# Softmax-free attention denominators: from two TensorE products with a head mask to 32x32 block transposes on VectorE

## The chip, the core and the metric

The kernel runs on one core of one Trainium2 chip. The metric is the time of one execution in microseconds (us), as the device reports it. The core has a matrix engine (TensorE, PE in the profile), VectorE (DVE), ScalarE (ACT), GpSimd (POOL) and SyncE (SP, which here only issues transfers). Each runs its own instructions in order, and they wait for each other through semaphores. PE reads SBUF and writes PSUM; the other compute engines work on tiles of 128 partitions by some number of columns.

## The reference, cut to what matters

x is 2048 tokens by 448 features. Two branches are computed from it and mixed by a gate per token.

```python
g = sigmoid((x * gate_w).sum(-1, keepdims=True))
# linear attention, 16 heads of 28
phi = lambda t: where(t > 0, t + 1, exp(t)) + 1e-6
pq, pk = phi(q), phi(k)                       # q, k, v from x @ wqkv
kv  = einsum("bhsd,bhse->bhde", pk, v)
z   = einsum("bhsd->bhd", pk)
num = einsum("bhqd,bhde->bhqe", pq, kv)
den = einsum("bhqd,bhd->bhq", pq, z)[..., None] + 1e-6
a   = (num / den) @ wo
# dense block, 1792 hidden
r = relu(x @ w1 + b1); b = (r * r) @ w2 + b2
out = g * a + (1 - g) * b
```

The change is about `den`: for each token and head, the sum over the 28 features of the head of pq times z, plus 1e-6, inverted, and then multiplied onto pq.

## The kernel before, in words

**Number format.** Every matrix product is made of two or three float32r products: each operand is split into a rounded high part and the rest (`split_hi` on line 63, mostly on ACT; `split_lo` on line 71, mostly on DVE), and high by high, high by low and low by high are accumulated in one PSUM bank. So each tensor that PE reads has passed an ACT copy and a DVE subtraction.

**Order.** PE, ACT and DVE run exactly in the order in which the program is written (line 170); a small list `todo` (`run_todo`, line 530) holds steps that are written one stage later than the products they follow. Tokens go in four blocks of 512 (TB); the hidden features in 14 chunks of 128, seven (NH) in a first half and seven in a second. The first half of the program runs blocks 0 to 3 over hidden chunks 0 to 6 together with the keys. The second half (line 684 on) runs blocks in the order 3, 0, 1, 2, which the loop calls n = 0 to 3, over hidden chunks 7 to 13, which it counts as fl = 0 to 6. In each stage (n, fl) PE does `up` (line 241: 11 products into `h_ps`), then `down` of the chunk before (line 260: 12 products into the four `o_ps` accumulators; `leave` holds back the last one or two of them until the next `down`), and then queries or attention. `hidden` (line 231) stands behind each `up`: ACT Relu and Square (`hr`), DVE cast (`hh`) and DVE subtraction (`hl`); `down` of that chunk one stage later needs `hh` and `hl`.

**Queries and denominators.** `queries(b, c)` (line 449) makes 128 rows of q per chunk c for 512 tokens: rows are features, columns tokens. Chunks 0 to 2 hold 24 features per head, chunk 3 the other four. A head has eight of the 128 rows in each chunk. Chunk 3 holds two partial sums per feature on separate partitions, which are swapped between partitions by eight small DMAs (`swap`, line 470, four issued on SP and four on POOL) and added (`join`, line 478). After phi (`qe`), the step `after` multiplies each row by its z (`zc`) and sums the four chunks into `ds`, 128x512: eight partial sums per head, one on each of the head's rows. From there:

- `split_den` (line 483): ACT rounds `ds` to `dh`, DVE subtracts to `dl`.
- `denominators` (line 489): PE multiplies the constant 128x128 mask `hm` (1 where two rows belong to one head) by `dh` and by `dl`, which leaves the head's sum on each of its eight rows (`d_ps`); ACT adds 1e-6 and copies to `rec`; DVE inverts `rec` by four reciprocals of 128 columns (line 498) in the stage after.
- `scaled(b, c)` (line 501): DVE multiplies `qe` by `rec` (line 506), ACT rounds to `qh`, DVE subtracts to `ql`. Chunk 3 goes through `split_last` (line 76).
- `attention` (line 513): 11 products per tile of 128 tokens, of `qh`, `ql` and `m_s` (kv times wo), into `a_ps`; ACT applies the gate (`u`), DVE adds to `part`.

For n = 0 `split_den` stands in stage 4 ahead of `up`, the mask products at the end of stage 4, the reciprocals at the head of stage 5, and `scaled` in stages 5 (chunk 0) and 6 (chunks 1 to 3). For n = 1 to 3 `split_den` and the mask products stand in stage 0, the reciprocals at the head of stage 1 ahead of `hidden`, and `scaled` in stages 2 and 3, two chunks each, one chunk after the other. Attention of block n = 0 comes in stage 0 of n = 1; that of the others in stages 4 to 6.

**Buffers.** `slot` (line 54) gives one of 15 SBUF buffers of 512 columns, `bank` (line 48) one of two PSUM banks in turn, for `k_ps`, `g_ps`, `q_ps`, `d_ps` and `a_ps` alike. `hm` comes from a mask that is loaded in the first half (lines 663 to 665).

Of the kernel before, what the change touches and what calls it, by code (L numbers as in the profile page):

```python
# [7 lines left out]
F = mybir.dt.float32  # L8
R = mybir.dt.float32r
AF = mybir.ActivationFunctionType  # L10
# [4 lines left out]
DH = D // H  # L15
# [13 lines left out]

@with_exitstack  # L30
def gated_mix_kernel(ctx: ExitStack, tc: tile.TileContext, xw, xt, xn, wk, wq, wv, wo, w1a, w1b, w2, b1, b2, gw,
                     hmask, kvmask, halves, out):
    nc = tc.nc
    act, dve, pool, pe, sp = nc.scalar, nc.vector, nc.gpsimd, nc.tensor, nc.sync

# [12 lines left out]
    def bank(name):  # L48
        turn[0] ^= 1
        return ms_p.tile([P, 512], F, name=name, tag=f"ms{turn[0]}")  # L50
# [3 lines left out]
    def slot(shape, dt, name):  # L54
        return work.tile(shape, dt, name=name, tag="s", bufs=NSLOT)

    def load(dst, src):
        sp.dma_start(out=dst, in_=src)
# [4 lines left out]
    def split_hi(eng, hi, src):  # L63
        if eng is act:
            act.activation(hi, src, AF.Copy)  # L65
        elif eng is pool:
            pool.tensor_scalar(hi, src, 1.0, 0.0, op0=ALU.mult, op1=ALU.add)
        else:
            eng.tensor_copy(hi, src)  # L69

    def split_lo(eng, lo, src, hi):
        eng.tensor_tensor(lo, src, f32(hi), op=ALU.subtract)  # L72
# [8 lines left out]
    def products(out_ps, terms):  # L81
        n = len(terms)
        for i, (a, b) in enumerate(terms):
            pe.matmul(out_ps, a, b, start=(i == 0), stop=(i == n - 1))  # L84
# [119 lines left out]

    b2_s = keep.tile([P, D], F, name="b2_s")
    gw_s = keep.tile([P, D], F, name="gw_s")
    hm = keep.tile([P, 8 + P], R, name="hm")[:, 8:]
    dve.memset(ones, 1.0)
    ksum = keep.tile([P, D], F, name="ksum")

# [146 lines left out]
    def split_wq(c):  # L357
        raw = wq_raw.pop(c)
        split_hi(act, wq_s[:, c], raw)
        if c < 3:  # L360
            split_lo(dve, wq_s[:, 4 + c, :384], raw[:, :384], wq_s[:, c, :384])
        else:
            split_lo(dve, wq_s[64:, 3, :384], raw[64:, :384], wq_s[64:, 3, :384])
        second = [t[:, 384:].rearrange("p (j r) -> p j r", j=NJ)[:, :, 16:] for t in (wq_s[:, c], raw)]
        split_lo(dve, second[0], second[1], second[0])


# [4 lines left out]
    def key_sums():  # L372
        zk = slot([P, 4, NJ, 32], F, "zk")
        ks = ksum.rearrange("p (j k) -> p j k", j=NJ)
        pool.memset(zk[:, 3], 0.0)
        pool.tensor_copy(zk[:, :3], ks[:, :, :96].rearrange("p j (c r) -> p c j r", c=3))
        pool.tensor_copy(zk[:, 3, :, :16], ks[:, :, 96:])
        zks.append(zk)
        act.activation(gate[:, 0], logit, AF.Exp, scale=-1.0)
        dve.tensor_scalar_add(gate[:, 0], gate[:, 0], 1.0)  # L380
        dve.reciprocal(gate[:, 0], gate[:, 0])
        dve.tensor_scalar(gate[:, 1], gate[:, 0], -1.0, 1.0, op0=ALU.mult, op1=ALU.add)
# [49 lines left out]
    def m_product(j):  # L432
        wh, wl = wo_s.pop(j)
        ps = mm_p.tile([P, 512], F, name=f"m_ps{j}", tag="mm")
        products(ps[:, :D], [(kv[0][:, j], wh), (kv[0][:, j], wl), (kv[1][:, j], wh)])
        m = late.tile([P, 2, D], R, name=f"m{j}", tag="m", bufs=1)
        split_hi(act, m[:, 0], ps[:, :D])
        split_lo(dve, m[:, 1], ps[:, :D], m[:, 0])

        p = j * 32  # L440
        for c in range(3):
            pool.dma_start(out=m_s[p:p + 32, c::4][:, :2], in_=m[c * 32:c * 32 + 32])
        pool.dma_start(out=m_s[p:p + 16, 3], in_=m[96:112, 0])
        pool.dma_start(out=m_s[p + 16:p + 32, 3], in_=m[112:, 1])


    pq, qs, den = {}, {}, {}
# [1 line left out]
    def queries(b, c):  # L449
        ps = bank(f"q_ps{b}_{c}")  # L450
        xh, xl = xs[b]
        cols = slice(c * P, (c + 1) * P)
        if c < 3:
            products(ps, terms_w(xh, xl, wq_s, cols))
        else:
            products(ps, [(wq_s[:, i, cols], x[:, i]) for i in range(4) for x in ((xh, xl) if i < 3 else (xh,))])
        e = slot([P, TB], F, f"qe{b}_{c}")
        r = slot([P, TB], F, f"qr{b}_{c}")
        v = slot([P, TB], F, f"qv{b}") if c == 3 else None
        pq[b, c] = e  # L460

        def after():
            phi(ps if c < 3 else v, e, r, e)
            if (b, "s") not in den:
                den[b, "s"] = slot([P, TB], F, f"ds{b}")
                dve.tensor_scalar(den[b, "s"], e, zc[:, c:c + 1], None, op0=ALU.mult)
            else:
                dve.scalar_tensor_tensor(den[b, "s"], e, zc[:, c:c + 1], den[b, "s"], op0=ALU.mult, op1=ALU.add)

        def swap():  # L470

            act.copy(v, ps)  # L472
            for p in range(0, P, 32):
                load(r[p:p + 16], v[p + 16:p + 32])
                pool.dma_start(out=r[p + 16:p + 32], in_=v[p:p + 16])  # L475
            return [join]

        def join():
            dve.tensor_tensor(v, v, r, op=ALU.add)
            after()  # L480
        return [swap if c == 3 else after]

    def split_den(b):
        den[b, "h"], den[b, "l"] = slot([P, TB], R, f"dh{b}"), slot([P, TB], R, f"dl{b}")
        total = den.pop((b, "s"))
        split_hi(act, den[b, "h"], total)
        split_lo(dve, den[b, "l"], total, den[b, "h"])

    def denominators(b):
        ps = bank(f"d_ps{b}")  # L490
        products(ps, [(hm, den.pop((b, "h"))), (hm, den.pop((b, "l")))])
        den[b, "r"] = rec = slot([P, TB], F, f"rec{b}")

        act.activation(rec, ps, AF.Copy, bias=1e-6)

        def part_(i):
            for j in range(2 * i, 2 * i + 2):
                dve.reciprocal(rec[:, j * P:(j + 1) * P], rec[:, j * P:(j + 1) * P])
        return [lambda: part_(0), lambda: part_(1)]

    def scaled(b, c):
        p = pq.pop((b, c))
        h = late.tile([P, TB], R, name=f"qh{b}_{c}", tag="q", bufs=NLATE)
        lo = late.tile([P, TB], R, name=f"ql{b}_{c}", tag="q", bufs=NLATE)
        qs[c] = (h, lo)
        dve.tensor_tensor(p, den[b, "r"], p, op=ALU.mult)
        if c < 3:
            split_hi(act, h, p)
            split_lo(dve, lo, p, h)
        else:  # L510
            split_last(h, lo, p, half)

    def attention(b, i):
        t = 4 * b + i
# [104 lines left out]
    for b in range(1, NB):  # L619
        for f in range(NH):  # L620
# [36 lines left out]
            if b == 2:  # L657
                if f < 4:
                    load_wq(f)
                if 1 <= f < 5:  # L660
                    split_wq(f - 1)
                if f == 5:
                    raw = slot([P, P], F, "hmr")
                    pool.dma_start(out=raw, in_=hmask)
                    split_hi(act, hm, raw)
                    load(half, halves)
            if b == 3:
                if f < 4:
# [18 lines left out]
    for n, b in enumerate(order):  # L687
        then = order[n + 1] if n + 1 < NB else None
        for f in range(NF - NH, NF):
            fl = f - NH  # L690
            run_todo()
            if fl == (0 if n else 4) and n != 1:
                split_den(b)
            up(b, f)
            if then is not None and n and fl < 2:
                load_x(then, 2 * fl)
                load_x(then, 2 * fl + 1)
# [21 lines left out]
            if fl:  # L719
                if n + 1 < NB or f + 2 < NF:  # L720
                    down(b, f - 1, leave=leaves[n][fl])
                elif f + 1 < NF:
                    down(b, f - 1, range(3))
                    down(b, f - 1, [3], leave=leaves[n][fl], end=NH - 3)
            elif n == 0:
                down(b, NH - 1)
                half_done(b)
            else:
                down(order[n - 1], NF - 1)
                for i in range(4):  # L730
                    if n == 1:
                        attention(order[0], i)
                        if i == 1:
                            split_den(b)
                    finish(order[n - 1], i)
            if n == 0:
                if fl in (2, 3):
# [14 lines left out]
                    m_product(2)  # L752
                if fl == 5:
                    m_product(3)
                for c in ((0,), (1, 2, 3))[fl - 5] if fl >= 5 else ():
                    scaled(b, c)
                if fl >= 4:
                    for c in ((3,), (0,), (1, 2))[fl - 4]:
                        todo += queries(then, c)
                if fl == 4:  # L760
                    todo += denominators(b)
            else:
                if fl == 0:
                    todo += denominators(b)
                if 2 <= fl < 4:
                    scaled(b, 2 * fl - 4)
                    scaled(b, 2 * fl - 3)
                for i in (((0,), (1,), (2, 3)) if then is not None else ((0, 1), (2,), (3,)))[fl - 4] if fl >= 4 else ():
                    attention(b, i)
                if then is not None and 3 <= fl:  # L770
# [71 lines left out]
```

## Time and profile before

| what | value |
|---|---|
| time, median of 3 runs | 435.01 us |
| lowest and highest of them | 434.67 and 435.04 us |
| profiled execution, first to last instruction (its span) | 432.7 us |
| median less that span: start and end of the program | 2.3 us |
| granted TensorE clock in the profile | 1.000 |
| ACT busy, share of the span | 174.8 us, 40% |
| POOL busy, share of the span | 72.0 us, 17% |

The profile records the span of one execution and no time of its own around it; the 2.3 us are the difference to the median. "L254" is line 254 of the kernel; a line can be that of a helper, so tiles tell more than lines. Busy times of PE overlap, because a product is counted until its modelled end while the next is already running; the distance from start to start of two products is what one costs.

### The profile page before, as it was taken

What the parts mean: (1) busy time and instruction counts of PE and PEld (TensorE: products, weight loads), DVE (VectorE), ACT (ScalarE), POOL (GpSimd) and SP (SyncE); (2) the same over time, 40 slices, a digit from 0 to 9 for tenths busy, and PEclk for the clock granted to TensorE, in tenths of its full rate; (3) what the DMA queues carried; (4) which work ended last, traced back from release to release, by engine and by line L of the source; (5) the groups of instructions that cost most, each with busy time, mean ns of one, the idle gap of its engine ahead of it and who ended that gap; (6) DMA issues with size and microseconds to landing.
All of it is one profiled execution on the core that took longest, in us unless ns stands there. A gap on an engine that the chain in (4) does not pass through costs nothing.

```text
span 432.7 us, 5576 instructions
## 1 busy us (share of the span) xinstructions
PE 428.9 (99%) x2058; PEld 380.6 (88%) x2058; DVE 284.7 (66%) x464; ACT 174.8 (40%) x304; POOL 72.0 (17%) x93
## 2 busy tenths in 40 slices
PE   9999999999999999999999999999999999999997
PEld 6889999898989899898898888988888888888986
DVE  5999518843499337884459777887653966457624
ACT  6855324521346133453145543444433534233421
POOL 0055006500065002540010441000100001000000
PEclk9999999999999999999999999999999999999999
DMA  8842302120232211223245321130101401002002
GB/s 284 240 134 63 96 0 71 24 68 5 65 89 63 68 45 48 66 59 110 65 117 144 72 63 38 63 120 0 26 0 46 139 0 27 0 0 86 0 2 85
DMA packets 18411, 29.11 MB, mean 67 GB/s; under 512 B 2896, under 2 KB 12736, under 8 KB 18384
## 3 DMA queue, kind: packets, MB, share of 16 engines
q1 hardware_dynamic: 16480, 26.46, 20.1%
q0 software_dynamic: 1760, 2.20, 2.3%
q8 instruction: 16, 0.26, 0.3%
q14 instruction: 11, 0.09, 0.1%
q10 hardware_dynamic: 144, 0.10, 0.1%
HBM read 22.43 MB, written 3.67 MB: 60 GB/s over the span
## 4 chain that ended last, share of the span: by engine, by line
PE 99%; DVE 0%; issue 0%
PE h_ps L229 32%; PE o_ps L254 31%; PE q_ps L84 8%; PE a_ps L84 8%; PE g_ps L84 8%; PE k_ps L254 8%; PE kv_ps L404 1%; PE warm_ps L177 1%; PE m_ps L84 1%; PE d_ps L84 0%; PE last L84 0%; PE h_ps L549 0%; PE z_ps L398 0%; DVE last L786 0%
## 5 line engine op out<-in xcount | busy, mean ns | idle before, releaser
L254 PE MATMUL o_ps<-w,hh 128*128 128x448 f32 x444 | 127.9, 362 | 0.0
L229 PE MATMUL h_ps<-xh,w 128*128 128x512 f32 x390 | 124.7, 390 | 0.0
L254 PEld LDWEIGHTS o_ps<-w,hh 128*128 128x128 f32 x444 | 83.2, 187 | 7.6
L229 PE MATMUL h_ps<-xl,w 128*128 128x512 f32 x224 | 86.7, 389 | 0.0
L229 PEld LDWEIGHTS h_ps<-xh,w 128*128 128x128 f32 x390 | 73.1, 188 | 14.7 <-DVE w L72 0.4
L254 PE MATMUL o_ps<-w,hl 128*128 128x448 f32 x222 | 80.4, 362 | 0.0
L233 ACT ACTIVATE hr<-h_ps,b_s 128x512 f32<-128x512 f32 x56 | 38.1, 680 | 85.8 <-PE h_ps L229 80.3
L69 DVE CAST hh<-hr 128x512 fp32r<-128x512 f32 x56 | 23.5, 420 | 61.3 <-ACT hr L234 61.1
L229 PEld LDWEIGHTS h_ps<-xl,w 128*128 128x128 f32 x224 | 42.0, 188 | 7.9
L254 PEld LDWEIGHTS o_ps<-w,hl 128*128 128x128 f32 x222 | 41.6, 188 | 3.7
L72 DVE TENSOR_TENSOR hl<-hr,hh 128x512 fp32r<-128x512 f32 x56 | 39.6, 707 | 3.4
L72 POOL TENSOR_TENSOR nl<-xnr,nh 128x384 fp32r<-128x384 f32 x16 | 17.2, 1075 | 119.0 <-ACT nh L65 118.9
L234 ACT ACTIVATE hr<-hr 128x512 f32<-128x512 f32 x56 | 35.4, 632 | 1.8
L84 PE MATMUL q_ps<-xh,wq_s 128*128 128x512 f32 x100 | 33.0, 389 | 0.0
L84 PE MATMUL a_ps<-m_s,qh 128*128 128x448 f32 x112 | 32.7, 362 | 0.0
L254 PE MATMUL k_ps<-wk_s,xh 128*128 128x448 f32 x112 | 32.7, 361 | 0.0
L475 POOL DMA_DIRECT2D qr<-qv x16 | 7.9, 503 | 124.3 <-ACT qv L472 94.5
L72 DVE TENSOR_TENSOR pl<-r,ph 128x448 fp32r<-128x448 f32 x16 | 23.7, 1479 | 0.0
L326 POOL TENSOR_TENSOR ksum<-ksum,r 128x448 f32<-128x448 f32 x15 | 23.3, 1554 | 1.1 <-DVE r L288 1.1
L84 PE MATMUL q_ps<-xl,wq_s 128*128 128x512 f32 x60 | 23.3, 389 | 0.0
L254 PE MATMUL k_ps<-wk_s,xl 128*128 128x448 f32 x64 | 23.2, 363 | 0.0
L84 PE MATMUL a_ps<-m_s,ql 128*128 128x448 f32 x64 | 23.2, 362 | 0.0
(118 smaller groups left out, 571.0 us busy)
## 6 DMA issues: line engine op xcount, KB each, us to landing
xr<-in_xt SPq DMA_DIRECT2D x27, 256.0 KB, 2.7
xnr<-in_xn SPq DMA_DIRECT2D x16, 224.0 KB, 2.6
out<-out SPq DMA_DIRECT2D x15, 224.0 KB, 2.0
w2r<-in_w SPq DMA_DIRECT2D x14, 224.0 KB, 2.7
w1r<-in_w1a SPq DMA_DIRECT2D x7, 256.0 KB, 2.8
w1r<-in_w1b SPq DMA_DIRECT2D x8, 192.0 KB, 3.3
m_s<-m POOLq DMA_DIRECT2D x12, 112.0 KB, 2.5
wqr<-in_wq SPq DMA_DIRECT2D x4, 256.0 KB, 2.7
```

The costliest lines, as they stand in the source:

```text
L69: eng.tensor_copy(hi, src)
L72: eng.tensor_tensor(lo, src, f32(hi), op=ALU.subtract)
L84: pe.matmul(out_ps, a, b, start=(i == 0), stop=(i == n - 1))
L177: pe.matmul(warm_ps[:, :256], warm[:, :P], warm, start=True, stop=True)
L229: pe.matmul(ps, a, m, start=(c == 0 and n == 0), stop=(c == 3 and n == 1))
L233: act.activation(r, ps, AF.Relu, bias=b1_s[:, f:f + 1])
L234: act.activation(r, r, AF.Square)
L254: pe.matmul(ps, a, m, start=start, stop=stop)
L326: pool.tensor_tensor(ksum, ksum, p, op=ALU.add)
L404: pe.matmul(kv_ps[:JE, js], wv_s[c][:, js], gsum[c][:, js], start=(c == 0), stop=(c == 3))
L475: pool.dma_start(out=r[p + 16:p + 32], in_=v[p:p + 16])
```

## The change

The 128x512 sums `ds` are no longer sent through PE. One step, `denominators`, does all: DVE transposes `ds` in 32x32 blocks (tokens now lie on partitions, the 32 rows of a block in columns), adds up groups of eight neighbouring columns (512 columns to 64: 16 blocks by four heads), adds 1e-6 and inverts on those 64 columns; ACT copies each of them eight times; DVE transposes back into the buffer of `ds`, which `scaled` then reads as the inverse. For this the eight rows of a head must be neighbours, so the host lays out the columns of the weights in another order, and the pairs of chunk 3 lie on even and odd partitions: the swap DMAs, the last two copies of `m_product`, one copy of `key_sums` and a subtraction in `split_wq` go in steps of two instead of runs of 16. The mask, its load and its rounding go.

`split_den` goes. `denominators` stands at the end of stage 4 for n = 0, and in stage 1 behind `up` (and so behind `hidden`) for n = 1 to 3. `scaled` now takes a pair of chunks: the product of the second chunk is written ahead of the subtraction of the first. For n = 0 the pairs stand in stages 5 and 6.

```diff
-    def split_den(b):
-        den[b, "h"], den[b, "l"] = slot([P, TB], R, f"dh{b}"), slot([P, TB], R, f"dl{b}")
-        total = den.pop((b, "s"))
-        split_hi(act, den[b, "h"], total)
-        split_lo(dve, den[b, "l"], total, den[b, "h"])
-
     def denominators(b):
-        ps = bank(f"d_ps{b}")
-        products(ps, [(hm, den.pop((b, "h"))), (hm, den.pop((b, "l")))])
-        den[b, "r"] = rec = slot([P, TB], F, f"rec{b}")
-
-        act.activation(rec, ps, AF.Copy, bias=1e-6)
-
-        def part_(i):
-            for j in range(2 * i, 2 * i + 2):
-                dve.reciprocal(rec[:, j * P:(j + 1) * P], rec[:, j * P:(j + 1) * P])
-        return [lambda: part_(0), lambda: part_(1)]
-
-    def scaled(b, c):
-        p = pq.pop((b, c))
...
+        total, turned = den.pop((b, "s")), slot([P, TB], F, f"dt{b}")
+        dve.transpose(turned, total)
+        heads = total[:, :TB // 8]
+        dve.tensor_reduce(heads, turned.rearrange("p (h k) -> p h k", k=8), axis=mybir.AxisListType.X, op=ALU.add)
+        dve.tensor_scalar_add(heads, heads, 1e-6)
+        dve.reciprocal(heads, heads)
+        act.activation(turned.rearrange("p (h k) -> p h k", k=8), heads.unsqueeze(2).to_broadcast([P, TB // 8, 8]),
+                       AF.Copy)
+        den[b, "r"] = total
+        dve.transpose(total, turned)
+
+    def scaled(b, chunks):
+        owing = None
+        for c in chunks:
+            p = pq.pop((b, c))
...
+            dve.tensor_tensor(p, den[b, "r"], p, op=ALU.mult)
+            if owing:
+                split_lo(dve, *owing)
+            owing = None
+            if c < 3:
+                split_hi(act, h, p)
+                owing = lo, p, h
+            else:
+                split_last(h, lo, p, half)
+        if owing:
+            split_lo(dve, *owing)
...
             for p in range(0, P, 32):
-                load(r[p:p + 16], v[p + 16:p + 32])
-                pool.dma_start(out=r[p + 16:p + 32], in_=v[p:p + 16])
+                load(r[p:p + 32:2], v[p + 1:p + 32:2])
+                pool.dma_start(out=r[p + 1:p + 32:2], in_=v[p:p + 32:2])
...
-            if fl == (0 if n else 4) and n != 1:
-                split_den(b)
             up(b, f)
+            if n and fl == 1:
+                denominators(b)
...
-                for c in ((0,), (1, 2, 3))[fl - 5] if fl >= 5 else ():
-                    scaled(b, c)
+                if fl >= 5:
+                    scaled(b, ((0, 1), (2, 3))[fl - 5])
...
                 if fl == 4:
-                    todo += denominators(b)
+                    denominators(b)
             else:
-                if fl == 0:
-                    todo += denominators(b)
                 if 2 <= fl < 4:
-                    scaled(b, 2 * fl - 4)
-                    scaled(b, 2 * fl - 3)
+                    scaled(b, ((0, 1), (2, 3))[fl - 2])
...
-    head = 4 * (p // 32) + p % 16 // 4
+    head = p // 8
```

More of the change, by code (lines that the diff above doesn't have):

```diff
@@ L31, in gated_mix_kernel @@
 def gated_mix_kernel(ctx: ExitStack, tc: tile.TileContext, xw, xt, xn, wk, wq, wv, wo, w1a, w1b, w2, b1, b2, gw,
-                     hmask, kvmask, halves, out):
+                     kvmask, halves, out):
     nc = tc.nc
@@ L206, in gated_mix_kernel @@
     gw_s = keep.tile([P, D], F, name="gw_s")
-    hm = keep.tile([P, 8 + P], R, name="hm")[:, 8:]
+    keep.tile([P, 8 + P], R, name="off")
     dve.memset(ones, 1.0)
@@ L363, in split_wq @@
             split_lo(dve, wq_s[64:, 3, :384], raw[64:, :384], wq_s[64:, 3, :384])
-        second = [t[:, 384:].rearrange("p (j r) -> p j r", j=NJ)[:, :, 16:] for t in (wq_s[:, c], raw)]
+        second = [t[:, 385::2] for t in (wq_s[:, c], raw)]
         split_lo(dve, second[0], second[1], second[0])
@@ L376, in key_sums @@
         pool.tensor_copy(zk[:, :3], ks[:, :, :96].rearrange("p j (c r) -> p c j r", c=3))
-        pool.tensor_copy(zk[:, 3, :, :16], ks[:, :, 96:])
+        pool.tensor_copy(zk[:, 3, :, ::2], ks[:, :, 96:])
         zks.append(zk)
@@ L442, in m_product @@
             pool.dma_start(out=m_s[p:p + 32, c::4][:, :2], in_=m[c * 32:c * 32 + 32])
-        pool.dma_start(out=m_s[p:p + 16, 3], in_=m[96:112, 0])
-        pool.dma_start(out=m_s[p + 16:p + 32, 3], in_=m[112:, 1])
+        pool.dma_start(out=m_s[p:p + 32:2, 3], in_=m[96:112, 0])
+        pool.dma_start(out=m_s[p + 1:p + 32:2, 3], in_=m[112:, 1])
     pq, qs, den = {}, {}, {}
@@ L501, in scaled @@
-    def scaled(b, c):
-        p = pq.pop((b, c))
[L503 to L511, printed above, removed]
+    def denominators(b):
+        total, turned = den.pop((b, "s")), slot([P, TB], F, f"dt{b}")
[8 more added lines that the diff above has]
+        dve.transpose(total, turned)
@@ new lines, in scaled @@
+    def scaled(b, chunks):
+        owing = None
+        for c in chunks:
+            p = pq.pop((b, c))
+            h = late.tile([P, TB], R, name=f"qh{b}_{c}", tag="q", bufs=NLATE)
+            lo = late.tile([P, TB], R, name=f"ql{b}_{c}", tag="q", bufs=NLATE)
+            qs[c] = (h, lo)
+            dve.tensor_tensor(p, den[b, "r"], p, op=ALU.mult)
[9 more added lines that the diff above has]
+            split_lo(dve, *owing)
@@ L662, in gated_mix_kernel @@
                 if f == 5:
-                    raw = slot([P, P], F, "hmr")
-                    pool.dma_start(out=raw, in_=hmask)
-                    split_hi(act, hm, raw)
                     load(half, halves)
@@ L732, in gated_mix_kernel @@
                         attention(order[0], i)
-                        if i == 1:
-                            split_den(b)
                     finish(order[n - 1], i)
@@ L802 @@
     p = np.arange(P)
-    head = 4 * (p // 32) + p % 16 // 4
-    q_of = np.stack([head * DH + c * 8 + p % 32 // 16 * 4 + p % 4 for c in range(3)] + [head * DH + 24 + p % 4])
-    k_of = np.concatenate([np.r_[q_of[:3, 32 * j:32 * j + 32].reshape(-1), q_of[3, 32 * j:32 * j + 16]]
+    head = p // 8
+    q_of = np.stack([head * DH + c * 8 + p % 8 for c in range(3)] + [head * DH + 24 + p % 8 // 2])
+    k_of = np.concatenate([np.r_[q_of[:3, 32 * j:32 * j + 32].reshape(-1), q_of[3, 32 * j:32 * j + 32:2]]
                            for j in range(NJ)])
-    hmask = (head[:, None] == head[None, :]).astype(np.float32)
     kvmask = (np.arange(JE)[:, None] // DH == k_of[None, :] // DH % 4).astype(np.float32)
-    halves = np.where(p[:, None] % 32 < 16, [[-1.0, 0.0]], [[1.0, 1.0]]).astype(np.float32)
+    halves = np.where(p[:, None] % 2 == 0, [[-1.0, 0.0]], [[1.0, 1.0]]).astype(np.float32)
     w1 = inputs["B_w1"][twice].reshape(4, P, 2, NH * P).transpose(2, 0, 1, 3)
@@ L828 @@
         "gw": inputs["gate_w"],
-        "hmask": hmask,
         "kvmask": kvmask,
```

## The prediction

> **What bounds the kernel now.** I read the busy shares first, then the chain of work that ended last, on the page.
>
> ```profile
> span 432.7 us, 5576 instructions
> PE 428.9 (99%) x2058; PEld 380.6 (88%) x2058; DVE 284.7 (66%) x464; ACT 174.8 (40%) x304; POOL 72.0 (17%) x93
> ...
> PE 99%; DVE 0%; issue 0%
> ```
>
> The chain is PE from end to end: TensorE runs product behind product, and no step of the chain is a wait for another engine. DVE is busy for two thirds of the span and idle for one. So a product taken from PE's list is worth what it occupies there, as long as no other engine becomes late; what DVE or ACT gain or lose is worth nothing by itself. Next, the same chain in order of time, for the block n = 2, and the operations of the removed tile.
>
> ```profile
> 335.85 0.45 PE d_ps L84 x2
> ...
> 338.80 2.21 PE o_ps L254 x11
> 341.00 2.49 PE h_ps L229 x11
> 343.50 2.21 PE o_ps L254 x11
> 345.70 2.49 PE h_ps L229 x11
> 348.19 2.81 PE o_ps L254 x14
> ...
> 357.49 2.20 PE a_ps L84 x11
> ```
>
> ```profile
> L84 PE MATMUL d_ps<-dh,hm x4: 388/388/389, 250.8 to 388.3; 128*128 128x512 f32 x4
> ...
> L84 PE MATMUL d_ps<-dl,hm x4: 389/389/389, 251.1 to 388.5; 128*128 128x512 f32 x4
> ```
>
> The reader is to see that one mask product lasts 0.39 us, but a pair takes only 0.45 us of the chain, since products overlap; and that the pieces join without a gap (343.50 + 2.21 = 345.71, the next starts at 345.70).
>
> **What PE gives back.** There are four pairs, one per block: 4 x 0.45 = 1.8 us. All four stand between other products in PE's list, none at an end. The span of the profiled execution becomes 432.7 - 1.8 = 430.9 us. The median of the runs is 2.3 us above that span (435.0 - 432.7), which I leave as it is: 433.2 us. This is the whole gain; the rest of this part asks whether it is lost again.
>
> **What DVE and ACT lose and gain in a block.** The rows of the operations concerned, grouped by line with shapes apart (count, then busy us and mean ns):
>
> ```profile
> L72 DVE TENSOR_TENSOR dl<-ds,dh 128x512 fp32r<-128x512 f32 x4 | 2.8, 691 | 2.1 <-ACT dh L65 2.1
> L498 DVE RECIPROCAL rec<-rec 128x128 f32<-128x128 f32 x16 | 13.5, 908 | 0.9 <-ACT rec L494 0.9
> L381 DVE RECIPROCAL gate<-gate 128x16 f32<-128x16 f32 x1 | 0.3, 252 | 0.0
> L380 DVE TENSOR_SCALAR gate<-gate 128x16 f32<-128x16 f32 x1 | 0.2, 168 | 0.0
> L72 DVE TENSOR_TENSOR pl<-r,ph 128x448 fp32r<-128x448 f32 x16 | 23.7, 1479 | 0.0
> L65 ACT ACTIVATE dh<-ds 128x512 fp32r<-128x512 f32 x4 | 2.5, 630 | 6.9 <-DVE ds L468 6.9
> L494 ACT ACTIVATE rec<-d_ps 128x512 f32<-128x512 f32 x4 | 2.4, 597 | 3.5 <-PE d_ps L84 3.5
> L468 DVE SCALAR_TENSOR_TENSOR ds<-qe,zc,ds 128x512 f32<-128x512 f32 x12 | 9.0, 752 | 0.4
> ```
>
> ```profile
> 338.80 3.38 DVE L498 RECIPROCAL rec<-rec 128x128 f32<-128x128 f32 x4
> 342.09 0.36 DVE L69 CAST hh<-hr 128x512 fp32r<-128x512 f32 x1
> 342.49 0.69 DVE L72 TENSOR_TENSOR hl<-hr,hh 128x512 fp32r<-128x512 f32 x1
> 343.10 1.28 DVE L72 TENSOR_TENSOR xl<-xr,xh 128x512 fp32r<-128x512 f32 x2
> ```
>
> Removed per block: the subtraction `dl` (0.69 us) and four reciprocals (3.38 us) on DVE, the rounding `dh` (0.63 us) and the copy `rec` (0.60 us) on ACT. Added, none of it in this trace but the kinds of the two small ones:
>
> - Two transposes and one reduction, each passing 512 columns. The nearest rows with 512 columns at both ends are the cast (0.36 us) and the subtraction (0.69 us); the slowest DVE pace of the trace is the reciprocal's, (908 - 252) / 112 = 5.9 ns a column, or about 3.2 us for 512. I take 0.69 us for each, as the commonest pace of this shape, and keep 0.36 and 3.2 us as ends.
> - The addition on 64 columns: 0.17 us, from 16 columns. The reciprocal on 64: 0.25 + 48 x 5.9 ns = 0.53 us.
> - ACT's copy from 64 columns to 512: 0.60 us as `rec`, at worst the 1.14 us that the timeline below has for two roundings of this width.
>
> A dependent DVE operation starts 0.04 us after its predecessor (342.09 + 0.36 to 342.49). So the chain is 0.69 + 0.69 + 0.17 + 0.53 + 0.60 + 0.69 with five gaps of 0.04, 3.6 us, of which DVE works 2.8 and waits for ACT 0.7. DVE had spent 4.1 us on the same task. By my values the work off PE shrinks a little.
>
> [...]
>
> **Who could become late: stage 2 of n = 1 and 2.** The chain now stands behind `hidden` of stage 1; queued behind it are, on ACT, two roundings of the next x and the Relu of stage 2, and on DVE the x subtractions and the cast of stage 2. PE waits for that cast in its next `down`. The ACT rows of the same stretch:
>
> ```profile
> 338.83 0.69 ACT L233 ACTIVATE hr<-h_ps,b_s 128x512 f32<-128x512 f32 x1 [1.89 <-PE h_ps L229]
> 339.55 0.63 ACT L234 ACTIVATE hr<-hr 128x512 f32<-128x512 f32 x1
> 340.09 1.14 ACT L65 ACTIVATE xh<-xr 128x512 fp32r<-128x512 f32 x2
> 343.53 0.69 ACT L233 ACTIVATE hr<-h_ps,b_s 128x512 f32<-128x512 f32 x1 [2.31 <-PE h_ps L229]
> ```
>
> I set the new order on the old clock of PE. Square of stage 1 ends at 339.55 + 0.63 = 340.2; the cast, no longer behind the reciprocals, and the subtraction end at 341.3. The chain: transpose to 342.1, reduction to 342.8, addition to 343.0, reciprocal to 343.6, ACT's copy to 344.2, transpose back to 344.9. ACT goes on with the two roundings to 345.4, Relu and Square of stage 2 to 346.8, and DVE ends the cast at 347.2 and the subtraction at 347.9. PE's `down` of that chunk is the piece at 348.19 with 14 products; its first two are held back from the chunk before (`leave` is 2), so at 0.20 us each (2.21 / 11) it needs the cast at 348.6 and the subtraction, for the third product, at 349.0. **The margin is 1.1 us**, say 1.0. Before, Relu began at 343.53 and Square (0.63 us) and cast (0.4) followed at once, so that the cast ended near 345.3, over 3 us early: the change uses up most of that cover. In the stages after this, one pair of chunks follows each `hidden`; with the old durations the subtraction of the last chunk ends at about 357.9.
>
> ```profile
> 357.99 0.69 DVE L72 TENSOR_TENSOR ql<-qe,qh 128x512 fp32r<-128x512 f32 x1
> ```
>
> Before, it ended at 358.7. PE reads it with the eleventh product of the attention piece at 357.49, at 359.5: 0.8 us spare before, 1.6 after. For n = 3 there is no next x to round, which gives 1.14 us more: margin 2.1 us.
>
> **Stage 4 to 6 of n = 0.** Here the chain runs on a DVE that is nearly full until the attention of the next stage. The tightest place is a bank: the first attention product needs the bank of the query chunk read at 273.22.
>
> ```profile
> 273.22 0.68 DVE L287 TENSOR_SCALAR qr<-q_ps 128x512 f32<-128x512 f32 x1
> ```
>
> ```profile
> 274.43 3.60 PE a_ps L84 x18
> ```
>
> ```profile
> DVE ql L72 <- ACT qh L65: 8.4, 12, 0.7
> ...
> DVE qh L78 <- ACT ql L77: 3.2, 4, 0.8
> ...
> DVE dl L72 <- ACT dh L65: 2.1, 3, 0.7
> ```
>
> The bank was free 0.5 us ahead of PE. The waits view (us in total, times, longest) shows what pairing can save: 0.7 us of DVE idleness in every chunk of `scaled`, about 2 us in a block once the second product fills it. With `dl`, its wait of 0.7 and the reciprocals gone (4.8 us) and 3.6 added, DVE arrives about 3 us earlier, PE 0.45: margin some 3 us. Removing one use of `bank` moves every later use to the other of two banks; each still waits for the use before last, and the mask products were nobody's only cover.
>
> **Edits that I cost at nothing.** The swap DMAs in steps of two: the last of four SP issues ends at 307.5 and lands 2.2 us later, at 309.7, and the addition that needs it starts at 312.18; 2.5 us cover them, a doubled landing too.
>
> ```profile
> 305.05 2.42 SPq L58 DMA_DIRECT2D qr<-qv  x4
> ```
>
> ```profile
> qr<-qv SPq DMA_DIRECT2D x16, 32.0 KB, 2.2
> ```
>
> ```profile
> 312.18 0.69 DVE L479 TENSOR_TENSOR qv<-qv,qr 128x512 f32<-128x512 f32 x1
> ```
>
> The strided copies of `m_product`, `key_sums` and `split_wq` keep their counts and sizes. The mask's load and rounding went beside PE. Two slots per block fewer are taken, so no buffer comes free later.
>
> **The rivals.**
>
> *The chain is too slow for its place, and the kernel gets slower.* If transposes and reduction run at the 1.48 us that a subtraction of 448 columns takes in the first half (row `pl`), the chain is 3 x 0.79 = 2.4 us longer. PE then waits 1.4 us in stage 2 of n = 1 and of n = 2, 0.3 of n = 3, and not for n = 0: 3.1 us lost against 1.8 gained, 436.3 us. It decides from 1.9 us over my chain on, where 2 x 0.9 eats the gain. At the reciprocal's pace (3 x 2.5 = 7.5 us over) it would be 6.5 + 6.5 + 5.4 + 4.5 less 1.8, some 456 us. For it speaks that no row shows these operations; against it, that everything on DVE but the reciprocal and the operations of the first half passes 512 columns in 0.75 us or less (row `ds`). [...] Chance 0.13.
>
> *Part is lost:* 1.2 to 1.7 us over, two waits of 0.2 to 0.7 us, 433.6 to 434.6 us; 0.07, mostly still below 434.1.
>
> *PE reaches the next wait earlier and no more.* Each block brings PE 0.45 us nearer to the last `ql`, where it had 0.8; if that `ql` came 0.8 us later than before rather than 0.8 earlier, 0.45 a block would go and the time stay at 435.0. It needs the pairing to save nothing. 0.04.
>
> **How the numbers follow.** Forecast 433.2 us, chance 0.76. A difference of 0.2% (0.87 us) is about what a measurement of this kernel can tell from no change. Faster by more than that: the forecast and 0.06 of the partial loss, 0.82; within: 0.05; slower: 0.13. The three runs before spread by 0.4 us and the forecast itself may be off by 0.3; the range goes up through the partial loss to 434.4 and down to 432.6, which leaves the slow rival and the lost gain out, 0.17 to 0.18.
>
> **What would show it.** In the profile after: a PE chain of 99% with no `d_ps`, 8 products fewer, span 430.9; transposes and reduction near 0.69 us; no wait of PE for `hh` or `hl` in stage 2. It is wrong if one of the three lasts over 1.2 us, if ACT's copy waits long enough that the Relu behind it comes over a microsecond later than I put it, or if PE shows gaps ahead of `o_ps` or `a_ps`.

## The result and the profile after

The changed kernel takes 433.06 us (median of 5 runs, 432.92 to 433.26) against 435.04 us before (5 runs, 434.67 to 435.20). The ratio is 0.9956, with a 95% interval from 0.9945 to 0.9967: 1.4 to 2.4 us less. The forecast was 433.2 us.

The page of the changed kernel, in the lines that answer to those shown of before:

```profile
span 431.1 us, 5536 instructions
...
PE 427.1 (99%) x2050; PEld 379.3 (88%) x2050; DVE 280.6 (65%) x464; ACT 172.4 (40%) x299; POOL 71.6 (17%) x92
...
PE 98%; DMA 1%; ACT 0%; SPq 0%; DVE 0%; issue 0%
```

PE has 2050 products instead of 2058 and still fills the span; DVE has as many instructions as before (464) and 4.1 us less work. Where the time went is read by laying the chains in order of time side by side: `up` of stage 4 of n = 0, ahead of the first pair of mask products, and then `up` of stage 1 in the three other blocks, each just behind one more pair. Before:

```profile
244.11 2.49 PE h_ps L229 x11
...
283.68 2.49 PE h_ps L229 x11
...
336.30 2.49 PE h_ps L229 x11
...
388.92 2.49 PE h_ps L229 x11
```

After:

```profile
244.35 2.49 PE h_ps L229 x11
...
283.01 2.50 PE h_ps L229 x11
...
335.18 2.49 PE h_ps L229 x11
...
387.35 2.49 PE h_ps L229 x11
```

The changed kernel is 0.24 us late before anything of the change acts, and then 0.67, 1.12 and 1.57 us early: two pairs give 0.91 us, the third and the fourth 0.45 each, 1.81 in all. The 0.24 us come from the program's first loads. In this profile one of them is on the chain, ahead of the first products:

```profile
1.64 4.39 DMA xr<-in_xt
...
15.22 2.21 PE k_ps L254 x11
```

The product group that starts at 15.22 us here started at 14.98 before, and between 15.18 and 16.15 in the other profiles, of kernels that are the same up to there. So spans of single profiles differ by about a microsecond for a reason ahead of the change; the medians are what counts. The five runs of the changed kernel also show what lies between a span and its time: 1.8 us (432.92 us for a span of 431.1). Of the 2.3 us before, then, some 0.5 are not start and end of the program: the profiled execution was that much shorter than the median one.

The new operations of the changed kernel, grouped by line (count, busy us and mean ns, idle before):

```profile
L493 DVE STREAM_TRANSPOSE ds<-dt 128x512 f32<-128x512 f32 x4 | 2.8, 712 | 2.8 <-ACT dt L490 2.8
L485 DVE STREAM_TRANSPOSE dt<-ds 128x512 f32<-128x512 f32 x4 | 2.8, 704 | 0.0
L487 DVE TENSOR_REDUCE ds<-dt 128x64 f32<-128x512 f32 x4 | 2.7, 686 | 0.1
...
L489 DVE RECIPROCAL ds<-ds 128x64 f32<-128x64 f32 x4 | 2.2, 553 | 0.1
...
L488 DVE TENSOR_SCALAR ds<-ds 128x64 f32<-128x64 f32 x4 | 0.8, 196 | 0.1
```

```profile
L490 ACT ACTIVATE dt<-ds 128x512 f32<-128x512 f32 x4 | 2.5, 632 | 13.0 <-DVE ds L489 13.0
```

Each is what the prediction took for it, within 0.03 us. Stages 1 and 2 of n = 2, as DVE went through them:

```profile
339.10 0.43 DVE L69 CAST hh<-hr 128x512 fp32r<-128x512 f32 x1 [1.78 <-ACT hr L234]
339.56 0.69 DVE L72 TENSOR_TENSOR hl<-hr,hh 128x512 fp32r<-128x512 f32 x1
340.17 0.70 DVE L485 STREAM_TRANSPOSE dt<-ds 128x512 f32<-128x512 f32 x1
...
343.11 0.71 DVE L493 STREAM_TRANSPOSE ds<-dt 128x512 f32<-128x512 f32 x1 [0.70 <-ACT dt L490]
343.74 1.25 DVE L72 TENSOR_TENSOR xl<-xr,xh 128x512 fp32r<-128x512 f32 x2
345.38 0.43 DVE L69 CAST hh<-hr 128x512 fp32r<-128x512 f32 x1 [0.39 <-ACT hr L234]
345.92 0.69 DVE L72 TENSOR_TENSOR hl<-hr,hh 128x512 fp32r<-128x512 f32 x1
...
355.68 0.69 DVE L72 TENSOR_TENSOR ql<-qe,qh 128x512 fp32r<-128x512 f32 x1
```

and, in stage 3, the first products of the `down` that reads that last cast (`hh`, from the third product on) and subtraction (`hl`, the fifth):

```profile
346.91 0.37 PE L254 MATMUL o_ps<-w,hh 128*128 128x448 f32 x1
347.12 0.36 PE L254 MATMUL o_ps<-w,hl 128*128 128x448 f32 x1
347.32 0.56 PE L254 MATMUL o_ps<-w,hh 128*128 128x448 f32 x2
347.72 0.36 PE L254 MATMUL o_ps<-w,hl 128*128 128x448 f32 x1
```

The chain runs from 340.17 to 343.82, 3.65 us. The cast ends at 345.81 for a product at 347.32, 1.5 us early; the subtraction at 346.61 for 347.72, 1.1 us early. And DVE now stands 1.78 us in front of the first cast, waiting for Square, a time that the reciprocals used to fill. The two subtractions `xl` end at 344.99, against 344.38 before; PE is 1.12 us earlier here, so against PE they end 1.7 us later than before. The wait of 1.78 us matters below.

### The profile page after: what moved, and what is told of

Its sections match the earlier page's. It is cut to its first block, busy times and chain, and to the rows that moved or that the text cites. A ratio compares the mean times of both kernels' runs of the same rounds, so it can differ in the third digit from the quotient of the medians.

```text
span 431.1 us, 5536 instructions
## 1 busy us (share of the span) xinstructions
PE 427.1 (99%) x2050; PEld 379.3 (88%) x2050; DVE 280.6 (65%) x464; ACT 172.4 (40%) x299; POOL 71.6 (17%) x92
## 4 chain that ended last, share of the span: by engine, by line
PE 98%; DMA 1%; ACT 0%; SPq 0%; DVE 0%; issue 0%
PE h_ps L229 32%; PE o_ps L254 31%; PE q_ps L84 8%; PE g_ps L84 8%; PE k_ps L254 8%; PE a_ps L84 8%; DMA xr<-in_xt 1%; PE kv_ps L404 1%; PE m_ps L84 1%; PE last L84 0%; SPq L58 0%; PE z_ps L398 0%; ACT w L65 0%; ACT xh L65 0%; DVE last L779 0%
## 5 line engine op out<-in xcount | busy, mean ns | idle before, releaser
L527 DVE SCALAR_TENSOR_TENSOR part<-part,gate,u 128x448 f32<-128x448 f32 x16 | 10.9, 684 | 24.0 <-ACT u L526 24.0
L526 ACT ACTIVATE u<-a_ps,gate 128x448 f32<-128x448 f32 x16 | 10.1, 634 | 33.1 <-PE a_ps L84 33.1
```

Source lines behind the costliest of these rows:

```text
L526: act.activation(u, ps[:, :D], AF.Copy, scale=gate[:, 0, t:t + 1])
L527: dve.scalar_tensor_tensor(part[t], part[t], gate[:, 1, t:t + 1], u, op0=ALU.mult, op1=ALU.add)
```

## The experiments

**The theory**: the time is the room of the eight products in PE's list, 0.45 us a pair; everything on DVE and ACT is hidden, in stage 2 by about 1 us. **Rivals**: the gain, or part of it, comes from the lighter VectorE work or from the pairs of chunks; or the cover is thinner or thicker than I read it. Four kernels ran first: the products put back, the products alone left out, the pairs alone, and the layout alone.

**Products back.** The changed kernel with two products per block where the mask products stood:

```diff
+    def spare(b):
+        products(bank(f"sp_ps{b}"), [(wq_s[:, 0, :P], xs[b][0][:, 0])] * 2)
...
                 if fl == 4:
+                    spare(b)
                     denominators(b)
             else:
+                if fl == 0:
+                    spare(b)
```

> The changed kernel, with two products of 128x512 per block put back where the mask products stood; they multiply a piece of the query weights by x, wait for nothing new, and their result is read by nobody. If the gain is only the room of the eight products on TensorE (my theory), it goes: 433.1 + 4 x 0.45 = 434.9 us. If the gain came from the shorter work of VectorE and ScalarE or from the pairing of the scaled chunks (rival), the time stays near 433.1 us.

Measured: 435.00 us, ratio to before 1.0001 [0.9991, 1.0011]. The whole gain is gone, with all the new work on DVE in place. This is the theory's number. The spare products also take a turn of `bank` in each block, as the mask products did, so the turn of the banks is put back with them; in the chains of both kernels no product of the second half waits for a bank.

**Products left out.** The kernel before, with ACT reading `dh` in place of the products' result:

```diff
-        ps = bank(f"d_ps{b}")
-        products(ps, [(hm, den.pop((b, "h"))), (hm, den.pop((b, "l")))])
...
-        act.activation(rec, ps, AF.Copy, bias=1e-6)
+        act.activation(rec, f32(den.pop((b, "h"))), AF.Copy, bias=1e-6)
```

> The kernel before, with nothing but the eight mask products left out: ScalarE copies the rounded sums straight to the inverse's input, so the sum over a head's rows is left out of the computation; the four reciprocals, the rounding, the subtraction and the order stay as they were. Theory: 435.0 - 1.8 = 433.2 us, the whole gain without any of the new VectorE work. Rival (the old chain of reciprocals becomes the next thing TensorE waits for, so that the new chain was needed): 434 to 435 us.

Measured: 433.61 us, ratio 0.9968 [0.9955, 0.9980]. Most of the gain, but the median is 0.4 us above the theory's. The trace has a wait that neither kernel has, at the first attention product of stage 0 of n = 1:

```profile
275.12 0.68 PE L84 MATMUL a_ps<-m_s,qh 128*128 128x448 f32 x2 [0.26 <-DVE qr L287]
```

The view names 0.26 us, but by the starts of the products the loss is 0.5 us: this one follows 0.62 us behind its predecessor and the next 0.31 us behind it, where 0.20 is usual. That is about what the median lacks. This is the bank that the prediction called the tightest place: 0.5 us to spare before. PE is 0.45 us nearer to it once a pair is gone, and here DVE still has the old reciprocals and unpaired chunks.

**Pairs alone.** The kernel before with `scaled` of the changed kernel:

```diff
-                for c in ((0,), (1, 2, 3))[fl - 5] if fl >= 5 else ():
-                    scaled(b, c)
+                if fl >= 5:
+                    scaled(b, ((0, 1), (2, 3))[fl - 5])
...
-                    scaled(b, 2 * fl - 4)
-                    scaled(b, 2 * fl - 3)
+                    scaled(b, ((0, 1), (2, 3))[fl - 2])
```

> The kernel before, with only the scaled chunks in pairs as in the changed kernel; mask products, reciprocals and layout as before. Theory: VectorE gets some 2 us a block back and nobody on the chain waits for it, 435.0 us within 0.3. Rival (pairing is part of the gain): 434 us or less.

Measured: 434.99 us, ratio 0.9996 [0.9988, 1.0005]. Nothing, as the theory had it.

**Layout alone.** The kernel before with the host's new order of columns and all steps of two (`r[p:p + 32:2]` for `r[p:p + 16]` and so on):

> The kernel before, with only the new layout: a head's rows are neighbours, swap transfers and small copies go in steps of two, and the mask is that of the new layout. Theory: nothing on the chain changes, 435.0 us within 0.3. Rival (transfers between partitions in steps of two land later and delay the additions behind them): more than 435.5 us, and landings of the swap transfers well over 2.2 us.

Measured: 434.87 us, ratio 0.9997 [0.9988, 1.0007]. The landings of the swap transfers in this kernel:

```profile
qr<-qv SPq DMA_DIRECT2D x16, 32.0 KB, 2.2
qr<-qv POOLq DMA_DIRECT2D x16, 32.0 KB, 1.8
```

They were 2.2 and 1.9 us before. Steps of two between partitions cost these transfers nothing that the landings or the time show.

Then the cover was taken away piece by piece, in four kernels more.

**Products left out, and pairs.** The two edits above in one kernel, to see whether that wait was the missing piece.

> The kernel before without the eight mask products, as in the run that gave 433.6 us, and with the scaled chunks in pairs (the sum over a head's rows is left out of the computation here too). In that run TensorE waited 0.3 us for the bank of its first attention product, because VectorE came late with chunk after chunk. Theory: pairing gives VectorE about 2 us there, the wait goes, and the time is that of the changed kernel, 433.1 us. Rival (the rest of 0.5 us is the old chain's, or spread of the start): 433.6 us again.

Measured: 433.38 us (432.96 to 433.74), ratio 0.9963 [0.9951, 0.9976]. The wait is gone from the trace: PE's chain is without a gap, and the read of the bank that starts at 271.79 ends at 272.47, for a first product at 274.86. The median lies between the two expected values and its spread takes in both, so this run shows the wait gone, and its price only roughly.

**Unpaired.** The changed kernel with `scaled` called chunk by chunk as before (the diff of the pairs, turned round).

> The changed kernel with its scaled chunks one by one, and with one and three chunks in the last two stages of the first block, as before. Theory: in the changed kernel the bank that the first attention product needs is read 3.8 us ahead (from 269.75 + 0.68 to 274.22); without pairs some 2 us of that go, nothing waits, 433.1 us. Rival (the new chain is hidden only because the chunks are paired): 433.6 us or more, with a wait ahead of the attention products.

Measured: 435.39 us, ratio to before 1.0013 [1.0004, 1.0023]. **My expectation was wrong**: pairing, worth nothing by itself, is worth 2.3 us here. I had looked at the first block only. The waits are in stage 4 of n = 1 and n = 2, at the last chunk of the first attention piece (for n = 1):

```profile
305.85 0.37 PE L84 MATMUL a_ps<-m_s,ql 128*128 128x448 f32 x1
306.28 0.47 PE L84 MATMUL a_ps<-m_s,qh 128*128 128x448 f32 x1
307.00 0.47 PE L84 MATMUL a_ps<-m_s,ql 128*128 128x448 f32 x1 [0.25 <-DVE ql L72]
307.31 0.39 PE L84 MATMUL q_ps<-xh,wq_s 128*128 128x512 f32 x1
```

The piece and the one ahead of it are 1.1 us longer than without waits, in each of the two blocks. Starts must be read here, not the waits that the view names: it puts only 0.25 us down to `ql`, while two products follow 0.4 and 0.7 us behind their predecessors instead of 0.2. The last `ql` of n = 1 ends at 306.95 here; in the changed kernel it ends at 304.21, 1.8 us ahead of its product at 306.04. The four waits that DVE has again in `scaled`, 0.7 to 0.8 us for each chunk's rounding on ACT, make it 2.7 us later.

**A chain longer by three transposes, and by six.** In the changed kernel:

```diff
-        dve.transpose(turned, total)
+        for _ in range(4):          # 7 in the other
+            dve.transpose(turned, total)
```

> The changed kernel with the first transpose of each block done four times instead of once: VectorE's chain is longer by 3 x 0.61 to 3 x 0.73 = 1.8 to 2.2 us per block. Theory: in stage 2 of the second and third block the cast has 1.7 us and the subtraction 1.3 us to spare in the changed kernel's trace, so TensorE waits 0.5 to 0.9 us there and nowhere else: 434.1 to 434.9 us. Rival (VectorE is idle for a third of the span, so the work is hidden): 433.1 us.

Measured: 436.04 us, ratio 1.0024 [1.0015, 1.0033]: 3.0 us over the changed kernel, where I had expected 1.0 to 1.8. A repeated transpose costs 0.75 us (it waits for the one before), so the chain is 2.25 us longer. The cast and the subtraction of stage 2 of n = 1 on DVE, and the products of `down` in stage 3 that read them:

```profile
295.69 0.43 DVE L69 CAST hh<-hr 128x512 fp32r<-128x512 f32 x1 [0.39 <-ACT hr L234]
296.22 0.69 DVE L72 TENSOR_TENSOR hl<-hr,hh 128x512 fp32r<-128x512 f32 x1
```

```profile
295.18 0.37 PE L254 MATMUL o_ps<-w,hl 128*128 128x448 f32 x1
296.17 0.67 PE L254 MATMUL o_ps<-w,hh 128*128 128x448 f32 x2 [0.62 <-DVE hh L69]
296.96 0.47 PE L254 MATMUL o_ps<-w,hl 128*128 128x448 f32 x1
297.27 0.56 PE L254 MATMUL o_ps<-w,hh 128*128 128x448 f32 x2
```

The subtraction is read at 296.96 instead of 295.78, 1.2 us late for 2.25 us of delay: 1.05 us was spare. The expectation's 1.3 fits a count from the chain's piece; in the chain's view a piece starts where the one ahead of it ends, which is behind its first product (347.07 and 346.91 in the changed kernel). By the starts of the pieces the waits are 1.3 us for n = 1, 1.7 for n = 2 and 0.2 for n = 3. In n = 2 DVE also waited 0.42 us ahead of the chain for the buffer of `hl`, whose last user was an output transfer.

> The changed kernel with the first transpose of each block done seven times: 3.7 to 4.4 us longer per block, which is also what the rival of the prediction with slow transposes would look like. Theory: waits of 2.4 to 3.1 us in stage 2 of the second and third block, 1.3 to 2.0 in the last, up to 0.6 in the first: 6.1 to 8.8 us lost, 439 to 442 us. Rival (hidden): 433.1 us.

Measured: 446.66 us, ratio 1.0267 [1.0253, 1.0281]: 13.6 us over the changed kernel, far over the 6 to 9 I had expected. The first products of `down` in stage 3 of n = 1, which read the cast and subtraction of stage 2, and then three stretches of time behind the pause (length, busy us of PE with its products, of PEld, DVE, ACT and POOL, granted clock, transfers):

```profile
295.72 0.37 PE L254 MATMUL o_ps<-w,hl 128*128 128x448 f32 x1
298.94 0.67 PE L254 MATMUL o_ps<-w,hh 128*128 128x448 f32 x2 [2.86 <-DVE hh L69]
299.74 0.65 PE L254 MATMUL o_ps<-w,hl 128*128 128x448 f32 x1
300.18 0.95 PE L254 MATMUL o_ps<-w,hh 128*128 128x448 f32 x2
300.93 0.57 PE L254 MATMUL o_ps<-w,hl 128*128 128x448 f32 x1
301.30 0.95 PE L254 MATMUL o_ps<-w,hh 128*128 128x448 f32 x2
```

```profile
298.94:299.87 0.93, 0.80 (x3) 0.43 (x4) 0.88 (x2) 0.62 (x2) 0.00 (x0) 1.00 0.00 0
299.87:303.28 3.41, 3.41 (x10) 3.03 (x11) 3.28 (x6) 0.97 (x2) 0.00 (x0) 0.50 0.00 0
303.28:306.70 3.42, 3.42 (x17) 2.82 (x16) 2.83 (x6) 1.57 (x4) 0.00 (x0) 1.00 0.00 0
```

The cast comes 3.0 us late (298.94 instead of 295.92). But the piece loses 5.1 us: 0.4 us more are lost at the subtraction, and then three products take 1.12 us (300.18 to 301.30), 0.37 us each instead of 0.20, in a stretch of 3.41 us whose granted clock is 0.50. Half a clock for 3.41 us is 1.7 us lost. So a pause of 3 us cost 5. n = 2 lost 5.3 us in the same way, with a second stretch of 3.41 us at 0.50 (from 357.89; the mean granted clock from 350 to 365 us is 0.89); n = 3 lost 2.4 and n = 0 0.6, at the full clock. Without the two slow stretches some 10 us of waits are left, where the expectation had 6 to 9.

Three kernels settled what the unpaired run had left open.

**The chain ahead of `up`, unpaired.** In stage 1 of n = 1 to 3:

```diff
-            up(b, f)
             if n and fl == 1:
                 denominators(b)
+            up(b, f)
```

with `scaled` chunk by chunk:

> The changed kernel with chunks one by one, as in the run that gave 435.4 us, but with the chain of the second to fourth block ahead of up and hidden in stage 1, where the reciprocals stood. Theory: what the pairs make up for is the place of the chain: behind hidden it starts only after VectorE has stood 1.8 us waiting for Square; ahead of it the chain fills that wait, VectorE is some 1.5 us earlier in stage 2, and the 1.1 us that TensorE waited for the last chunk in the second and third block go: 433.1 to 433.4 us. Rival (the new chain itself is too long for unpaired chunks): 435.4 us again.

Measured: 433.05 us, ratio 0.9956 [0.9944, 0.9969], and no gap in PE's chain behind its first products. The last `ql` of n = 1 now ends at 305.36, 0.7 us ahead of its product at 306.07. With the chain at this place the pairs are not needed. So the 2.3 us of the unpaired run belong to the place of the chain and the single chunks together.

**The chain ahead of `up`, paired.**

> The changed kernel, pairs and all, with the chain of the second to fourth block ahead of up and hidden in stage 1. Theory: everything stays hidden, 433.1 us; the cast of stage 1 then waits for the chain and has 0.3 to 0.7 us to spare, that of stage 2 over 2.5 us. Rival (ScalarE's copy, which waits for the chain, now holds up the Relu of stage 1 and TensorE waits for its cast): 433.6 to 434.5 us, with waits ahead of the products of stage 2.

Measured: 433.29 us (433.00 to 433.51), ratio 0.9959 [0.9946, 0.9973]. Its trace has no wait in the second half either; it is the changed kernel's time. Nothing tried here beats the changed kernel beyond the spread of the runs.

**A chain longer by one transpose.**

> The changed kernel with the first transpose of each block done twice, 0.75 us more per block (the step measured in the run with three more). Theory: that run's waits put the spare time of the subtraction in stage 2 at 1.05 us, so 0.75 us costs nothing: 433.1 to 433.3 us. Rival (any lengthening of the chain is paid): 3 to 4 x 0.75 more, 435.3 to 436.1 us, or half of that if only two blocks pay.

Measured: 433.38 us (432.90 to 433.62), ratio 0.9961 [0.9949, 0.9974]. Nearly free, with one wait of 0.4 us in its profile, for the subtraction of stage 2 of n = 2. DVE had started the chain 0.64 us late there, for the same cause as above, and 0.64 + 0.75 is 0.3 us more than the 1.05 that are spare:

```profile
339.36 0.43 DVE L69 CAST hh<-hr 128x512 fp32r<-128x512 f32 x1 [1.77 <-ACT hr L234]
340.43 0.69 DVE L72 TENSOR_TENSOR hl<-hr,hh 128x512 fp32r<-128x512 f32 x1 [0.64 <-DMA out<-out]
```

## Why the prediction was right

**What PE gives back: right.** Four pairs at 0.45 us; the chain after is early by 0.91, 0.45 and 0.45 us at the places where the pairs were, and the products put back take all of it away. The 2.3 us between span and median were read wrongly as start and end of the program (1.8 us), but this does no harm: the forecast is the median less 1.8 us, whatever the span was.

**What the new operations cost: right.** Transposes 0.70 and 0.71 us for 0.69, reduction 0.69, reciprocal 0.55 for 0.53, addition 0.20 for 0.17, ACT's copy 0.63 for 0.60, the chain 3.65 us for 3.6. The reduction's 686 ns are the pace of the subtraction `dl` before (691 ns).

**The margins: right in stage 2, and elsewhere on the safe side.** The cast had 1.5 us to spare for 1.4 predicted, the subtraction 1.1 for 1.1. The last `ql` of n = 2 ends at 356.37 and is read by the eleventh product of the attention piece, which starts at 358.20: 1.8 us for 1.6. The bank in n = 0 was read 3.6 us ahead of its product (270.43 for 274.06) for "some 3". The prediction, too, counted from the starts of the chain's pieces, some 0.15 us behind the first product; against the products its margins are that much thinner.

**The slow rival: its price was near, its extreme left out the clock.** It said that 2.4 us more of chain cost 3.1 us; 2.25 us more cost 3.0. Some of that agreement is luck: by the prediction's margins 2.25 us would cost 2.7, and in n = 2 a buffer came 0.42 us late, which it did not have. Here it was the later, more exact-looking expectation of 1.0 to 1.8 that missed: it took the repeated transposes too short, the cover too thick, and no buffer to come late. For far longer chains the prediction reckoned waits one for one. With six transposes more (4.5 us) its margins give 10.9 us of waits, and some 10 were measured; the 3.4 us for the clock come on top.

**Where the reasons were incomplete.** The prediction said of DVE and ACT that what they gain or lose is worth nothing by itself, and set the pairs down as margin. That holds for each part alone; together they hold each other up. The chain moved behind `hidden`, where DVE first waits 1.78 us for Square, so that DVE's stage ends 1.7 us later though its work is less. It is the pairs that pay for this move: without them, 2.3 us are lost. The prediction's sentence that no buffer comes free later was also too sure: in stage 1 of n = 2 the subtraction `hl` takes a buffer that an output transfer must leave first. In the three lengthened kernels DVE waited 0.64, 0.42 and 0.22 us for it (with one, three and six transposes more). In the changed kernel's own profile it just did not wait: the transfer landed at 339.33 and the subtraction starts at 339.56. Before, the reciprocals stood ahead of the subtraction (342.49), over 3 us behind that landing (339.12). From issue to landing the transfer took between 2.0 and 4.5 us in these traces; why was not tried.

## What to carry to other kernels

When one engine's list fills the span, count what an edit removes from that list by the distance from start to start, not by durations (0.45 us for two products of 0.39), and ask of everything else only how early it is for its reader. Busy time removed from an idle engine is not cover gained: what counts is when its last piece ends, and a chain moved from ahead of a wait to behind it ends later though it is shorter (here 1.7 us later, against PE). And parts that measure as nothing alone can be each other's cover (the pairs: 434.99 us alone, 2.3 us in the changed kernel): test them out of the changed kernel as well as into the old one.

## What the hardware showed unasked

In these runs a pause of PE of 3 us cost some 2 us more than its length (5.1 us lost for 3.0, 5.3 for 3.2), and one of 2.0 us only 0.4 more (2.4). Behind waits of 0.8 and 1.2 us (n = 1 and n = 2 of the run with three more transposes) and of 2.0 us (n = 3 of the run with six more) the granted clock stayed at 1.00, and products were back at 0.20 us from the fourth on. Behind the waits of 3.0 and 3.2 us (n = 1 and n = 2 of the run with six more) the granted clock fell to 0.50, not at once but 0.9 and 1.4 us after the first product, for 3.41 us each time, and products ran at 0.37 us. No run has a wait between 2.0 and 3.0 us, and none shows why the clock fell where it did.
